# A third tile for the rows of a batch, another order of the first loads and scales, and one quarter's sums a quarter earlier

## The chip, the cores and the metric

The kernel runs on one core of one Trainium2 chip. The metric is the device time of one execution in microseconds (us), taken as the median of several runs. Beside it stands one execution recorded by the hardware profiler; all times inside the kernel come from that one, in us from the start of its span.

The engines are named as the profile names them: PE (TensorE) with PEld, its weight loads; DVE (VectorE); ACT (ScalarE); POOL (GpSimd); SP (SyncE), which issues most DMAs.

## The reference, cut to what matters

An RWKV-5 attention layer with a decaying state per head, and behind it a layer of eight experts of which each token uses one.

```python
batch, n_heads, seq, head_dim = (4, 8, 768, 48)
...
for t in range(S):
    kt, vt, rt = (k[:, :, t], v[:, :, t], r[:, :, t])
    cur = np.einsum('bhd,bhe->bhde', u[None] * kt, vt)
    y[:, :, t] = np.einsum('bhd,bhde->bhe', rt, state + cur)
    state = w[None, :, :, None] * state + np.einsum('bhd,bhe->bhde', kt, vt)
...
x = np.ascontiguousarray(attn_out.transpose(0, 2, 1, 3)).reshape(B * S, H * D)
...
logits = x @ w_gate
expert_idx = np.argmax(logits, axis=1)
...
for e in range(E):
    mask = expert_idx == e
    ...
    xe = x[mask]
    h = np.maximum(xe @ w1[e], 0.0)
    ye = h @ w2[e]
    out[mask] = gate_w[mask, None] * ye
```

There are 3072 tokens of 384 numbers, and each expert has 1024 hidden numbers. Everything is float32.

## The kernel before

**Attention.** The work is cut into 16 pairs: batch b and two heads, pair i = 4b + hp. A pair's 768 tokens are six chunks of 128. For each pair the kernel loads a tile `rk` (r and k, channels on partitions, three tiles in turn; `load_rk`, L91) and a tile `vk` (v and k, tokens on partitions, four tiles in turn; `load_vk`, L96). SP issues both. What is done with a pair:

- `scale` (L264, instruction at L266): DVE multiplies r and k by the powers of the decay in `TT`; the result is `RK`. `pairs` (L270, L272) multiplies r by k for the tokens' own term (`rp`), on POOL except for pair 0; `keys` (L274, L276) multiplies k in `vk` by the decay to the chunk's end (`Kd`), mostly on POOL.
- `p_own` (L279, PE at L285) sums `rp` with u, and `own_t` (L288, DVE at L289) turns the sums. `diag` (L300, ACT at L303) puts them on the diagonal of the score tiles `A`.
- `p_scores` (L291, PE at L297) multiplies keys by queries into the PSUM banks X01 and X23; `mask` (L305, DVE at L309 and L311) copies the half above the diagonal into `A`, in three pieces.
- `p_ds` (L315, PE at L320) makes each chunk's addition to the state from `Kd` and `vk`, `scan` (L323, DVE at L325) carries the state through the chunks, and `p_out` (L329, PE at L340 and L345) makes the output from `A`, `vk`, the states and `RK`. `out_t` (L348, ACT at L350) copies it to `yT`, `p_tr` (L356, PE at L358) turns it so that tokens stand on partitions, and `keep` (L361, ACT at L363 and L364) copies it into `xb`, the rows of a batch. There are two `xb` tiles (L252), taken in turn by batch.

When a batch is complete, `choose` (L368) picks each token's expert, `p_rank` and `slots` give the place among the expert's tokens, `gates` and `ids` finish the row, and `send` (L410, POOL at L412) writes rows from `xb` to the HBM tensor `rows` at those places, one chunk of 128 tokens at a time, spread over the next pairs by the table `sends` (L696 to L699). So a batch's `xb` is read by DMAs during the four pairs after it, while the next batch fills the other tile. A batch's pairs reach `keep` two pairs late: batch 2's first rows (pair 8) are kept in step 10.

The order on each engine is the order in which the program text issues its instructions; each engine works its own list off in that order and waits on semaphores. The steps are written out by hand: pair 0 in L701 to L731, then the loop over i from L732. In a step, PE runs own tokens, scores, p_tr of i-2, p_ds of i, and p_out of i-1. `turn` (a copy of one number on POOL) makes POOL wait for DVE's `scale` or `own_t` before it goes on. `p_fill` (L107) multiplies an identity by itself; its result is used by nobody.

**First loads.** L103 to L105 issue r, k and v, k of pairs 0, 1, 2 in the order rk0, vk0, rk1, vk1, rk2, vk2, after the small tile `wug` (L78).

**Experts.** After the last pair, each expert's tokens are loaded from `rows`. Two small early passes take the first 160 tokens of experts 0 and 1; eight late passes k = 0 to 7 take the rest (widths in L36). From k = 2 on, the first matrix product is done in a form with fewer products: `quarter` (L486) computes a quarter of the hidden units from five sums of weights per quarter, which `quarter_sums` (L533) makes on DVE, and from four sums of tokens, which `token_sums` (L544) makes. `quart[q]` is one tile per quarter, shared by all passes. The second product of pass k-1 runs after the first of pass k: `L2` (L554) for the tokens past the first 256, and `tokens_out` (L586) for the first 256, again with sums (`inner_sums`, `weight_sums`). `tokens_out` begins with four small DVE operations at L589 to L594, which make the places `it2` to which the rows are scattered (L675). Its products go to PSUM banks in turn; the last one writes the bank that the first one used, so it waits for `add(so[1], ...)` (L621).

The loop over passes (L895) mixes these by hand. While pass k >= 2 runs its quarters q, DVE also makes the sums of the next pass's quarter q-2 (L923 and L924); those of quarters 2 and 3 follow after the pass, behind `xT` and `token_sums` of the next one (L928 to L932):

```python
                    if q > 1:
                        late[k + 1].quarter_sums(q - 2)
...
            if ahead:
                late[k + 1].token_sums()
                for q in range(0 if k == 1 else 2, 4 if k < n - 2 else 3):
                    late[k + 1].quarter_sums(q)
```

Of the kernel before, what the change touches and what calls it, by code (L numbers as in the profile page):

```python
# [11 lines left out]
I32 = mybir.dt.int32  # L12
# [28 lines left out]
def bc(ap, shape):  # L41
    return ap.to_broadcast(shape)


def straight(tc, rk, vk, w, w1, w2, out, flag):
# [45 lines left out]
    def load_rk(i):  # L91
        if i < U:
            b, hp = divmod(i, HP)
            nc.sync.dma_start(rks[i % 3][0:KP], rk[b, hp].rearrange("h p u s -> (h p) u s")[0:KP])

    def load_vk(i):  # L96
        if i < U:
            b, hp = divmod(i, HP)
            nc.sync.dma_start(vks[i % 4], vk[b, hp])

    ident = cp.tile([128, 128], FP32, name="ident")
    make_identity(nc, ident)
# [146 lines left out]
    Ss = [ca.tile([128, D, G - 1], FP32, name=f"S{i}") for i in range(2)]  # L249
    own = [ca.tile([128, G, 32], FP32, name=f"own{i}") for i in range(2)]  # L250
    yTs = [ca.tile([128, 2, S // 2], FP32, name=f"yT{i}") for i in range(3)]
    xbs = [ca.tile([128, G, HP, Q], FP32, name=f"xb{i}") for i in range(2)]  # L252
    lg, sub, ex, eq = [ca.tile([128, G, E], FP32, name=n) for n in ("lg", "sub", "ex", "eq")]
    rko = ca.tile([128, G, E], FP32, name="rko")
    mx, se, m2 = [ca.tile([128, G], FP32, name=n) for n in ("mx", "se", "m2")]
# [5 lines left out]

        return c + 4 * h if c < 4 else 8 + 2 * h + c - 4

    def scale(i):  # L264
        hp, x = i % HP, rks[i % 3]
        nc.vector.tensor_tensor(RKs[i % 3][0:KP].rearrange("p u (c t) -> p u c t", t=C),  # L266
                                x[0:KP].rearrange("p u (c t) -> p u c t", t=C),
                                bc(TT[:, hp, :, None, :], [KP, 2, G, C]), op=ALU.mult)

    def pairs(i, eng=None):  # L270
        x = rks[i % 3]
# [88 lines left out]

    def keep(i):  # L361
        b, hp = divmod(i, HP)
        nc.scalar.copy(xbs[b % 2][:, 0:4, hp, :], trv[0])  # L363
        nc.scalar.copy(xbs[b % 2][:, 4:G, hp, :], trv[1])  # L364

    full = [128, G, E]

    def choose(b):  # L368
        oh = ohs[b % 2]
        nc.vector.tensor_reduce(lg, xbs[b % 2][:, :, :, 2 * D:].rearrange("p c a e -> p c e a"), axis=AX, op=ALU.add)  # L370
        nc.vector.tensor_reduce(mx, lg, axis=AX, op=ALU.max)
        nc.vector.tensor_tensor(sub, lg, bc(mx[:, :, None], full), op=ALU.subtract)
        nc.scalar.activation(ex, sub, func=ACT.Exp)

        nc.vector.scalar_tensor_tensor(out=eq, in0=sub, scalar=0.0, in1=bc(rev[:, None, :], full),
                                       op0=ALU.is_equal, op1=ALU.mult)
        nc.vector.tensor_reduce(m2, eq, axis=AX, op=ALU.max)
        nc.vector.tensor_tensor(oh, eq, bc(m2[:, :, None], full), op=ALU.is_equal)
# [10 lines left out]
                             skip_group_check=True)  # L389

    def slots(b):
        oh, xb = ohs[b % 2], xbs[b % 2]
        nc.vector.tensor_tensor(rko, rp, oh, op=ALU.mult)
        with nc.allow_low_precision("whole numbers below 2^24"):
            nc.vector.tensor_reduce(slot[b % 2], rko, axis=AX, op=ALU.add)

    def gates(b):
        xb = xbs[b % 2]
# [11 lines left out]
    def send(b, cs):  # L410
        for c in cs:
            s_ = nc.gpsimd.indirect_dma_start(  # L412
                out=rows[:, :], out_offset=bass.IndirectOffsetOnAxis(ap=slot[b % 2][:, c:c + 1], axis=0),
                in_=xbs[b % 2][:, c].rearrange("p a q -> p (a q)"), in_offset=None, bounds_check=E * N - 1, oob_is_err=False)
            tc.declare_no_dep(s_.ins, group="rows", reason="each token has a row of its own")
            tc.add_to_no_dep_group("rows", s_.ins)

    def ids(b):
        nc.gpsimd.iota(xbs[b % 2][:, :, :, 2 * D + 1].bitcast(I32), pattern=[[4 * C, G], [1, HP]], base=4 * S * b,
                       channel_multiplier=4)  # L420

    def p_count():
# [18 lines left out]
    class Pass:  # L441
# [144 lines left out]
        def tokens_out(self):  # L586

            nt, it2 = self.nt, self.it2
            nc.vector.tensor_scalar(out=vt[:, 0:nt], in0=pos2[:, 0:nt], scalar1=float(self.s0),  # L589
                                    scalar2=bp[:, self.k:self.k + 1], op0=ALU.add, op1=ALU.is_lt)  # L590
            nc.vector.memset(it2[:, 0:nt], 1 << 20)
            nc.vector.tensor_scalar(out=ia[:, 0:nt], in0=self.xg[:, 0:nt, 1].bitcast(I32), scalar1=2, scalar2=None,  # L592
                                    op0=ALU.logical_shift_right)
            nc.vector.copy_predicated(it2[:, 0:nt], vt[:, 0:nt], ia[:, 0:nt])  # L594

# [16 lines left out]
            def Sm(k):  # L612
                return lambda f: sums[k][:, f, :]
# [17 lines left out]
            def weigh(o, x, t):  # L631
                nc.scalar.activation(o, x, func=ACT.Copy, scale=g[:, t])
# [171 lines left out]
    nc.gpsimd.tensor_copy(turn, xbs[1][0:1, G - 1, 2, 0:1])  # L804
    send(B - 2, range(3, G))
    p_out(U - 1)
    out_t(U - 1)
# [86 lines left out]

    for k, p in enumerate(late):  # L895
        o = late[k - 1]
        ahead = k + 1 < n and k > 0
        if k == n - 1:
            o.inner_sums()
# [10 lines left out]
        else:  # L910

            if k < 2:
                if k:
                    o.inner_sums()
                for f in range(FT):
                    p.L1((f,))
                    if f % 2:
                        result(p, f)
            else:
                for q in range(4):  # L920
                    p.quarter(q)
                    o.inner_sums((q,))
                    if q > 1:  # L923
                        late[k + 1].quarter_sums(q - 2)  # L924
                    if k == 2 and q % 2:
                        result(p, 2 * q - 1)
                p.relus()
            late[k + 1].xT()  # L928
            if ahead:
                late[k + 1].token_sums()  # L930
                for q in range(0 if k == 1 else 2, 4 if k < n - 2 else 3):
                    late[k + 1].quarter_sums(q)  # L932
            if k == 0:
                okay()
# [528 lines left out]
```

## Time and profile before

| What | Value |
|---|---|
| Median of 3 runs | 373.71 us (371.86 to 374.47) |
| The profiled execution, its own time | 367.2 us |
| Its span | 365.3 us |
| PE busy | 353.3 us, 97% of the span |
| DVE busy | 261.5 us, 72% |
| POOL busy | 204.6 us, 56% |
| ACT busy | 142.7 us, 39% |
| Granted PE clock | 0.996 |
| HBM read and written | 53.29 MB and 11.40 MB, 177 GB/s over the span |

How to read the profile lines: in a timeline a line has start, duration, engine, source line, operation, written tile <- read tiles, the shape, and how many instructions of the kind were merged; in square brackets stands how long the engine had been idle and what ended that wait. Ends of matrix products are modelled, so their start and the distance between weight loads are the better measure. A line of the DMA view has the tensor, the queue, the number of issues, the size of one and the time from issue to landing. SPq is the issue of a DMA by SP and no work of an engine.

The attention part ends at about 118 us, the early passes at about 142 us, and the late passes fill the rest.

### The profile page before, as it was taken

The page shows a single profiled execution, that of the slowest core. Times are in us where ns is not written, and L with a number is a line of the kernel's source. Part 1 is how long each engine was busy: PE and PEld are TensorE (multiplying, and loading weights), DVE is VectorE, ACT ScalarE, POOL GpSimd, SP SyncE. Part 2 cuts the span into 40 slices and gives each one's busy share as a digit, 9 for nine tenths or more (in the row PEclk, how much of TensorE's full clock was granted, in tenths as well). Part 3 has the DMA queues.
Part 4 walks back from the last instruction along what each step waited for, and adds up shares of the span by engine and source line. Part 5 has one row for each costly group of instructions (what it writes and reads, how often), then busy time and mean ns, then how long its engine had stood idle before and what let it go on. Part 6 is the DMA issues. An engine that isn't in the chain of part 4 may idle for free.

```text
span 365.3 us, 9077 instructions
## 1 busy us (share of the span) xinstructions
PE 353.3 (97%) x3355; PEld 335.1 (92%) x3355; DVE 261.5 (72%) x653; ACT 142.7 (39%) x411; POOL 204.6 (56%) x242
## 2 busy tenths in 40 slices
PE   8999999999999999999999999999999999999991
PEld 8788888878889999999999999999999999999891
DVE  6988798887872258675797994896788688685531
ACT  2688787777784301323213312312221231122210
POOL 5389889898864521642107308805912941999341
PEclk9999999999999999999999999999999999999998
DMA  7999999986566974988358237525842943313301
GB/s 211 272 253 241 282 255 264 255 249 195 212 170 203 316 282 99 245 257 217 126 178 196 88 92 200 159 86 168 191 129 93 210 148 127 102 51 108 126 20 50
DMA packets 35205, 65.08 MB, mean 178 GB/s; under 512 B 18617, under 2 KB 19657, under 8 KB 35152
## 3 DMA queue, kind: packets, MB, share of 16 engines
q1 hardware_dynamic: 29648, 49.86, 50.3%
q0 software_dynamic: 3776, 9.84, 7.6%
q10 hardware_dynamic: 1728, 4.72, 3.7%
q8 instruction: 28, 0.46, 0.6%
q14 instruction: 25, 0.20, 0.2%
HBM read 53.29 MB, written 11.40 MB: 177 GB/s over the span
## 4 chain that ended last, share of the span: by engine, by line
PE 90%; DVE 2%; POOL 2%; issue 2%; DMA 1%; POOLq 0%; ACT 0%; DVEq 0%
PE X L501 12%; PE X L563 10%; PE X L479 8%; PE tr L603 7%; PE yps L603 7%; PE X L297 6%; PE yps L340 6%; PE yps L501 5%; PE tr L358 5%; PE yps L345 3%; PE tr L501 3%; PE dsb L501 3%; PE dsb L603 3%; PE yps L563 2%; PE dsb L320 2%
## 5 line engine op out<-in xcount | busy, mean ns | idle before, releaser
L675 POOL DMA_INDIRECT out_dram<-yo,ix x28 | 28.4, 1013 | 68.0 <-DVE ia L592 63.8
L303 ACT ACTIVATE A<-ident,own 128x128 f32<-128x128 f32 x192 | 57.9, 390 | 7.0 <-DVE own L289 6.6
L412 POOL DMA_INDIRECT rows<-xb,slot x24 | 30.3, 1262 | 12.0 <-issue 4.8
L563 PE MATMUL X<-hT,w2s 128*128 128x160 f32 (+5 forms) x288 | 36.5, 287 | 0.0
L563 PEld LDWEIGHTS X<-hT,w2s 128*128 128x128 f32 x288 | 36.2, 191 | 0.2
L603 PE MATMUL yps<-tums,sums 128*128 128x192 f32 x184 | 32.4, 326 | 0.0
L603 PEld LDWEIGHTS yps<-tums,sums 128*128 128x128 f32 x184 | 30.3, 190 | 0.0
L675 POOL DMA_INDIRECT out_dram<-yt,it x16 | 16.8, 1048 | 22.1 <-DVE so L621 10.9
L272 POOL TENSOR_TENSOR rp<-rk 112x768 f32<-112x768 f32 x15 | 28.8, 1919 | 0.0
L266 DVE TENSOR_TENSOR RK<-rk,TT 112x1536 f32<-112x1536 f32 x16 | 27.8, 1735 | 1.1 <-DMA rk<-in_rk_dram 0.9
L297 PEld LDWEIGHTS X<-RK 48*128 48x128 f32 x384 | 23.1, 187 | 5.3 <-issue 4.3
L297 PE MATMUL X<-RK 48*128 48x128 f32 x384 | 27.1, 283 | 0.2 <-DVE RK L266 0.2
L309 DVE COPY_PREDICATED A<-strict,X 128x512 f32<-128x512 int32 x32 | 23.3, 742 | 5.0 <-ACT A L303 4.9
L501 PE MATMUL X<-xT,w1s 128*128 128x208 f32 (+5 forms) x120 | 26.0, 331 | 0.0
L689 POOL TENSOR_TENSOR tums<-w2s,tums 128x384 f32<-128x384 f32 x24 | 24.7, 1031 | 0.4
L340 PE MATMUL yps<-A,vk 128*48 128x128 f32 x384 | 24.0, 274 | 0.0
L501 PEld LDWEIGHTS X<-xT,w1s 128*128 128x128 f32 x120 | 20.9, 190 | 0.0
L340 PEld LDWEIGHTS yps<-A,vk 128*48 128x48 f32 x384 | 20.2, 123 | 0.5
L637 ACT COPY so<-tr 128x192 f32<-128x192 f32 x7 | 2.2, 318 | 44.4 <-PE tr L603 44.4
L689 DVE TENSOR_TENSOR sums<-hT 128x512 f32<-128x512 f32 x16 | 17.1, 1066 | 3.2 <-ACT hT L481 3.2
L603 PE MATMUL tr<-w2s,hT 128*128 128x192 f32 x112 | 19.4, 326 | 0.0
L530 ACT ACTIVATE hT<-hT 128x416 f32<-128x416 f32 (+5 forms) x23 | 12.3, 536 | 17.9 <-DVE hT L522 17.8
(214 smaller groups left out, 828.2 us busy)
## 6 DMA issues: line engine op xcount, KB each, us to landing
w1s<-in_w_dram SPq DMA_DIRECT2D x36, 384.0 KB, 3.2
rk<-in_rk_dram SPq DMA_DIRECT2D x16, 672.0 KB, 10.2
w2s<-in_w_dram SPq DMA_DIRECT2D x24, 384.0 KB, 3.8
vk<-in_vk_dram SPq DMA_DIRECT2D x16, 528.0 KB, 5.6
w2s<-in_w_dram ACTq DMA_DIRECT2D x8, 384.0 KB, 5.6
xs<-rows SPq DMA_DIRECT2D x16, 169.0 KB, 5.3
w1s<-in_w_dram ACTq DMA_DIRECT2D x4, 384.0 KB, 3.3
rows<-zt SPq DMA_DIRECT2D x1, 1248.0 KB, 8.9
```

What stands on the lines that cost most here:

```text
L266: nc.vector.tensor_tensor(RKs[i % 3][0:KP].rearrange("p u (c t) -> p u c t", t=C), x[0:KP].rearrange("p u (c t) -> p u c t", t=C), bc(TT[: ...
L272: (eng or nc.gpsimd).tensor_tensor(rps[i % 2][0:KP], x[0:KP, 0], x[0:KP, 1], op=ALU.mult)
L297: nc.tensor.matmul(o, lhsT=r[q, 1, c * C:(c + 1) * C], rhs=r[q, 0, c * C:(c + 1) * C], start=True, stop=True, skip_group_check=True)
L303: nc.scalar.activation(A[:, place(c, h), :], ident, func=ACT.Copy, scale=own[i % 2][:, c, h:h + 1])
L340: nc.tensor.matmul(o(c, h), lhsT=v[:, c, h * D:(h + 1) * D], rhs=A[:, place(c, h), :], start=c < 2, stop=c == 0, skip_group_check=True)
L412: s_ = nc.gpsimd.indirect_dma_start(out=rows[:, :], out_offset=bass.IndirectOffsetOnAxis(ap=slot[b % 2][:, c:c + 1], axis=0), in_=xbs[b % ...
L479: nc.tensor.matmul(p[:, 0:self.n], lhsT=w1s[self.k % 2][f // 2][:, m, f % 2 * 128:(f % 2 + 1) * 128], rhs=self.t[:, m, 0:self.n], start=m ...
L501: nc.tensor.matmul(p[:, at * n:(at + 1) * n], lhsT=a, rhs=b, start=j == 0, stop=j == len(ab) - 1, skip_group_check=True)
L563: nc.tensor.matmul(p[:, 0:n], lhsT=w2s[self.k % 2][f // 2][:, f % 2, m * 128:(m + 1) * 128], rhs=self.h[:, f, self.c:self.n], start=f == 0 ...
L603: nc.tensor.matmul(p[:, at * Z:(at + 1) * Z], lhsT=a(f), rhs=b(f), start=f == 0, stop=f == FT // 2 - 1, skip_group_check=True)
L675: s_ = nc.gpsimd.indirect_dma_start(out=to[:, :], out_offset=bass.IndirectOffsetOnAxis(ap=at, axis=0), in_=x, in_offset=None, bounds_check ...
L689: (eng or nc.vector).tensor_tensor(o, a, b, op=how)
```

## The change

- **Rows of a batch.** `xb` has three tiles instead of two, and a batch takes tile b % 3.
- **First loads.** rk0 is loaded by two DMAs, each with half of the tokens; the order is rk0 (two halves), rk1, vk0, rk2, vk1, vk2.
- **Start of pair 0 and 1.** `scale(0)` is done in two halves, and the scores of the first two chunks are issued after the first half. The scores of chunks 4 and 5 move ahead of the last key decays. `scale(1)` stands ahead of `keys(0)` on DVE, so behind `own_t(0)`. The first two masks of pair 0 stand ahead of `scan(0)`. The fills are 12 instead of 17, and 6 and 3 around `p_ds(0)` instead of 8 behind the scores.
- **Sums of a quarter.** In pass k = 2 alone the next pass's sums of quarter q-1 (not q-2) follow quarter q, so only those of quarter 3 stay behind the pass.
- **Places.** In every `tokens_out` the four small operations for `it2` are issued behind `so[3]` and its two weighings, not at the beginning.

```diff
     def load_rk(i):
...
-            nc.sync.dma_start(rks[i % 3][0:KP], rk[b, hp].rearrange("h p u s -> (h p) u s")[0:KP])
+
+            for q in (slice(0, S // 2), slice(S // 2, S)) if not i else (slice(0, S),):
+                nc.sync.dma_start(rks[i % 3][0:KP, :, q], rk[b, hp].rearrange("h p u s -> (h p) u s")[0:KP, :, q])
...
-    for i in range(3):
-        load_rk(i)
-        load_vk(i)
+    load_rk(0)
+    load_rk(1)
+    load_vk(0)
+    load_rk(2)
+    load_vk(1)
+    load_vk(2)
...
-    p_fill(17, X01[1][:, 0, :])
+    p_fill(12, X01[1][:, 0, :])
...
-    xbs = [ca.tile([128, G, HP, Q], FP32, name=f"xb{i}") for i in range(2)]
+    xbs = [ca.tile([128, G, HP, Q], FP32, name=f"xb{i}") for i in range(3)]
...
-    def scale(i):
+    def scale(i, c0=0, c1=G):
         hp, x = i % HP, rks[i % 3]
-        nc.vector.tensor_tensor(RKs[i % 3][0:KP].rearrange("p u (c t) -> p u c t", t=C),
-                                x[0:KP].rearrange("p u (c t) -> p u c t", t=C),
-                                bc(TT[:, hp, :, None, :], [KP, 2, G, C]), op=ALU.mult)
+        nc.vector.tensor_tensor(RKs[i % 3][0:KP].rearrange("p u (c t) -> p u c t", t=C)[:, :, c0:c1],
+                                x[0:KP].rearrange("p u (c t) -> p u c t", t=C)[:, :, c0:c1],
+                                bc(TT[:, hp, :, None, :], [KP, 2, c1 - c0, C]), op=ALU.mult)
...
-        nc.scalar.copy(xbs[b % 2][:, 0:4, hp, :], trv[0])
-        nc.scalar.copy(xbs[b % 2][:, 4:G, hp, :], trv[1])
+        nc.scalar.copy(xbs[b % 3][:, 0:4, hp, :], trv[0])
+        nc.scalar.copy(xbs[b % 3][:, 4:G, hp, :], trv[1])
...
             weigh(so[4], so[3], 0)
             weigh(so[5], so[3], 1)
+            places()
             product(bd, 0, Sm(3), B_(1, 1))
...
-    scale(0)
+    scale(0, 0, G // 2)
+    p_scores(0, range(2))
+    scale(0, G // 2, G)
     pairs(0, nc.vector)
     key_decay(0, HP)
     state_decay()
-    p_scores(0, range(2))
     p_own(0)
...
-    keys(0, nc.vector)
     diag(0)
+    p_scores(0, range(4, G))
     p_key_decay(1, HP - 1)
     load_rk(3)
     scale(1)
+    keys(0, nc.vector)
+    p_fill(6, yps[0][:, 384:512])
     nc.gpsimd.tensor_copy(turn, RKs[1][0:1, 0, 0:1])
     pairs(1)
     keys(1)
     p_ds(0)
-    scan(0)
     mask(0, 0)
     mask(0, 1)
-    p_scores(0, range(4, G))
+    scan(0)
     mask(0, 2)
-    p_fill(8, yps[0][:, 384:512])
+    p_fill(3, yps[0][:, 384:512])
...
+        lag = 1 if k == 2 else 2
...
-                    if q > 1:
-                        late[k + 1].quarter_sums(q - 2)
+                    if q >= lag:
+                        late[k + 1].quarter_sums(q - lag)
...
-                for q in range(0 if k == 1 else 2, 4 if k < n - 2 else 3):
+                for q in range(0 if k == 1 else 4 - lag, 4 if k < n - 2 else 3):
                     late[k + 1].quarter_sums(q)
```

`places` is the block of L589 to L594, made a function and called where the diff shows it.

More of the change, by code (lines that the diff above doesn't have):

```diff
@@ L369, in choose @@
         oh = ohs[b % 2]
-        nc.vector.tensor_reduce(lg, xbs[b % 2][:, :, :, 2 * D:].rearrange("p c a e -> p c e a"), axis=AX, op=ALU.add)
+        nc.vector.tensor_reduce(lg, xbs[b % 3][:, :, :, 2 * D:].rearrange("p c a e -> p c e a"), axis=AX, op=ALU.add)
         nc.vector.tensor_reduce(mx, lg, axis=AX, op=ALU.max)
@@ L391, in slots @@
     def slots(b):
-        oh, xb = ohs[b % 2], xbs[b % 2]
+        oh, xb = ohs[b % 2], xbs[b % 3]
         nc.vector.tensor_tensor(rko, rp, oh, op=ALU.mult)
@@ L397, in gates @@
     def gates(b):
-        xb = xbs[b % 2]
+        xb = xbs[b % 3]
         nc.vector.tensor_reduce(se, ex, axis=AX, op=ALU.add)
@@ L413, in send @@
                 out=rows[:, :], out_offset=bass.IndirectOffsetOnAxis(ap=slot[b % 2][:, c:c + 1], axis=0),
-                in_=xbs[b % 2][:, c].rearrange("p a q -> p (a q)"), in_offset=None, bounds_check=E * N - 1, oob_is_err=False)
+                in_=xbs[b % 3][:, c].rearrange("p a q -> p (a q)"), in_offset=None, bounds_check=E * N - 1, oob_is_err=False)
             tc.declare_no_dep(s_.ins, group="rows", reason="each token has a row of its own")
@@ L418, in ids @@
     def ids(b):
-        nc.gpsimd.iota(xbs[b % 2][:, :, :, 2 * D + 1].bitcast(I32), pattern=[[4 * C, G], [1, HP]], base=4 * S * b,
+        nc.gpsimd.iota(xbs[b % 3][:, :, :, 2 * D + 1].bitcast(I32), pattern=[[4 * C, G], [1, HP]], base=4 * S * b,
                        channel_multiplier=4)
@@ L588, in tokens_out, with places @@
             nt, it2 = self.nt, self.it2
[L589 to L594, printed above, removed]
+            def places():
+                nc.vector.tensor_scalar(out=vt[:, 0:nt], in0=pos2[:, 0:nt], scalar1=float(self.s0),
+                                        scalar2=bp[:, self.k:self.k + 1], op0=ALU.add, op1=ALU.is_lt)
+                nc.vector.memset(it2[:, 0:nt], 1 << 20)
+                nc.vector.tensor_scalar(out=ia[:, 0:nt], in0=self.xg[:, 0:nt, 1].bitcast(I32), scalar1=2, scalar2=None,
+                                        op0=ALU.logical_shift_right)
+                nc.vector.copy_predicated(it2[:, 0:nt], vt[:, 0:nt], ia[:, 0:nt])
             h, ws, g = self.h, w2s[self.k % 2], self.xg[:, :, 0:1]
@@ L803, in straight @@
     keep(U - 2)
-    nc.gpsimd.tensor_copy(turn, xbs[1][0:1, G - 1, 2, 0:1])
+    nc.gpsimd.tensor_copy(turn, xbs[(B - 1) % 3][0:1, G - 1, 2, 0:1])
     send(B - 2, range(3, G))
```

## The prediction

> **What bounds the kernel now.** I read the page first (busy shares, then the chain that ended last), then the timeline of three places that the diff touches, then the landings of the first loads.
>
> ```profile
> PE 353.3 (97%) x3355; PEld 335.1 (92%) x3355; DVE 261.5 (72%) x653; ACT 142.7 (39%) x411; POOL 204.6 (56%) x242
> ...
> PE 90%; DVE 2%; POOL 2%; issue 2%; DMA 1%; POOLq 0%; ACT 0%; DVEq 0%
> ```
> TensorE works 353.3 of 365.3 us and carries 90% of the chain. Only its 12 us of holes can be won, and an edit on another engine pays only where it closes one. Three holes lie near the diff.
>
> Hole 1, the end of pass k=2 (timeline):
> ```profile
> 189.88 1.46 PE L603 MATMUL tr<-tums,sums 128*128 128x192 f32 x8
> ...
> 191.60 0.22 DVE L589 TENSOR_SCALAR vt<-pos,bp 128x2 int32<-128x2 f32 x1
> ...
> 192.01 0.35 DVE L621 TENSOR_TENSOR so<-dsb,so 128x192 f32<-128x192 f32 x1
> ...
> 192.51 1.54 PE L603 MATMUL dsb<-tums,hT 128*128 128x192 f32 x8 [1.16 <-DVE so L621]
> ```
> The last product overwrites bank dsb, which VectorE reads only at 192.01, because two quarters' sums (five operations each, 189.33 to 190.45 and on to 191.6) and four small operations (191.60 to 192.01) stand ahead of that read.
>
> Hole 2, pair 10:
> ```profile
> 78.47 0.33 ACT L364 COPY xb<-X 128x208 f32<-128x208 f32 x1 [2.04 <-DMA rows<-xb,slot]
> ...
> 78.69 0.86 ACT L350 COPY yT<-yps 112x384 f32<-112x384 f32 x2
> 79.23 1.12 PEld L358 LDWEIGHTS tr<-sel,yT 112*128 112x128 f32 x8 [0.74 <-ACT yT L350]
> 79.23 1.29 PE L358 MATMUL tr<-sel,yT 112*128 112x104 f32 x8 [0.55 <-ACT yT L350]
> ```
> Batch 2 writes the xb tile that batch 0 is still sending from; ScalarE waits for that DMA, and TensorE behind it.
>
> Hole 3, the start. The chain passes through POOL: rp at 13.24, then TensorE's own tokens at 15.11.
> ```profile
> 13.24 1.82 POOL L272 TENSOR_TENSOR rp<-rk 112x768 f32<-112x768 f32 x1
> ...
> 15.03 1.19 POOL L276 TENSOR_TENSOR Kd<-vk,T 128x480 f32<-128x480 f32 x1
> ...
> 17.09 0.66 PE L320 MATMUL dsb<-vk,Kd 128*48 128x48 f32 x20
> ...
> 21.11 1.77 DVE L266 TENSOR_TENSOR RK<-rk,TT 112x1536 f32<-112x1536 f32 x1
> 21.23 3.35 POOL L272 TENSOR_TENSOR rp<-rk 112x768 f32<-112x768 f32 x1
> ```
> To see: POOL's product takes 1.82 alone, but 3.35 when it starts just after VectorE's scale: it stands still until that ends (22.88). The loads issued at 2.67 (vk1) and 3.68 (rk2):
> ```profile
> rk<-in_rk_dram SPq DMA_DIRECT2D x1, 672.0 KB, 11.9
> vk<-in_vk_dram SPq DMA_DIRECT2D x1, 528.0 KB, 10.3
> ```
> So vk1 lands at 12.97 and rk2 at 15.58. Windows of 1 us show the DMA share at 0.94 to 1.13 from 3 us on: the queue is full, and what goes ahead pushes back what follows.
>
> [...] The trace agrees (3.35 against 1.82; the turn copies of 1.55 to 1.62 under L266 against 0.18). [...] The packet records agree: 21 ns at least for 416 bytes, 119 for 3072, 232 for 6144. [...] Here the first fill's weight loads stand 0.213 us apart until 7.58 and 0.112 after.
>
> **One quarter's sums sooner (with the small operations moved): -1.40 us.** For k=2 the lag is 1: the sums of quarter q-1 follow quarter q. Behind quarter 3 stands one set where two stood around the transposes: minus five operations, 189.33 to 190.45, 1.12 us. The four small operations go behind so[3]: minus 0.41. The read of dsb moves from 192.01 to 190.48, ends at 190.83, before the product ahead ends (191.34). The hole closes: weight loads of that product and the next start 2.76 us apart (189.72, 192.48), of which 1.30 is the normal distance (188.42 to 189.72), less 0.06 that the next is shorter: 1.40. After that TensorE is its own limit: the last final of the pass then ends near 193.5, and the next quarter's first midu isn't due before 194.1. The moved set is done after quarter 1, at 177.09, under quarter 2: it delays midu from 177.32 to about 178.2, whose next reader waited for TensorE until 179.01, so it is free; without that cover it would cost 1.12. Its weights need no new wait: the last issue of that load is at 159.3. The small operations behind so[3] lie in 0.35 to 0.64 us of idle time ahead of the next final, in the other passes too: 0. Bounds: 1.1 to 1.5.
>
> **Three xb tiles: -0.78 us.** Without the DMA, L364 waits for the mask that ends at 77.16, as in pair 6 (mask to 51.57, copy at 51.65): 77.24 for 78.47. L350 then ends by 78.4, and L358 starts behind the scores at 78.61, as in pair 6 to 7 (scores 51.92, L358 53.02). Saved 79.23 - 78.61 = 0.62, plus 0.16 as L358 to L320 took 1.67 there and 1.51 in pair 7. Check: pair 11 lasts 7.44 (scores 77.59 to 85.03), pair 7 6.55, less 0.11 for the count: 0.78. At pair 14 the copy waited for the mask too (103.57), so nothing is won. Bounds: 0 to 0.9. Moved addresses: nothing of the next pool starts before all sends land (134.80), as before.
>
> **The start: +0.65 us.** Two DMAs for one on SP's queue: 0.42 us more of issue ahead of the rest, done by some 5.1, before any is needed; rk3's issue only waits for rp(0), 8.7 for 9.43, in a queue that is full anyway. Packets of 1536 bytes: by the records 8.8 ns + bytes/27.4, four cost 26 ns more than one of 6144; 7 rows per engine make 0.18 us. Step by step:
> - Half of rk0 lands near 5.5 (6.71 less half of the 2.5 us between landings), tables ready 5.87: scale from 5.9 for 6.80, but halves cost 2 x 0.9 for 1.76 and the second lands near 6.9. rp ends 8.72 (9.43), own tokens 9.73 (10.44): 0.7 sooner.
> - rk1 is now second, landing near 9.4: scale(1) 9.65 to 11.4 (13.04). vk0 lands near 11.3: keys(0) to 12.0; [...] POOL's rp(1) runs 12.1 to 13.95 (15.06): 1.1 sooner. Masks, scan, last mask to 14.6; own tokens to 15.0; scale(2), rk2 there since 13.8, 14.9 to 16.65.
> - But vk1 now stands behind rk2: as many bytes ahead as rk2 had, so 15.58 + 0.18 = 15.75. keys(1) on POOL, ready at 15.03 before, [...] 16.65 to 17.85. p_ds(1) starts at 17.9 (17.09). Behind it on POOL: the turn copy, rp(2) (to 19.85) and keys(2); on TensorE p_out(0). From p_ds to the next own tokens it is 2.73 us (23.49 to 26.22): 20.63 for 19.98, a loss of 0.65. Later pairs are bound by TensorE (6.22 each), so it stays.
> - Fewer fills (12 for 17, 6 + 3 for 8) are hidden: TensorE waits anyway. Unknown: whether the array, its fill ending at 6.56, still doubles its clock at 7.58. I take yes, as the scores follow by 6.9; if not, its doubled work until 17.9 is mostly waited for anyway: up to 1 us more. Bounds: -1.0 (vk1 by 14.1, as the first engines brought rk2) to +1.6.
>
> **Sum.** -1.40 - 0.78 + 0.65 = -1.53 us on the profiled execution of 367.2 (span 365.3): 365.7. The median of the runs is 6.5 above it; the same distance gives 372.2.
>
> **Rivals.**
> 1. The start wins: vk1 lands [...] (by 14.9), or POOL is not held. For it: rp(1) is 1.1 us sooner. Against: the full queue. Then -0.3 to -1.0, say -0.6: 370.9.
> 2. The third tile does nothing, another wait ending at the same time: 373.0. Against: pair 6.
> 3. Slower: the half packets hold the queue. Lateness of vk1 is free until 16.65, 0.9 us, then counts in full; the gains are gone at 2.4 us of delay (vk1 at 18.2), and beyond, say 3.5 us, it gives 374.8. Against: 0.18 by the packet records.
>
> **Chances.** Forecast 0.64 (own range 371.2 to 373.2), rival 1 0.22, rival 2 0.08, rival 3 0.03, a cold array 0.03 (373.2). The runs of before spread over 2.6 us; with a third of that (0.9) at each end I go from 370.9 - 0.9 to 373.0 + 0.9: 370.0 to 373.9. Faster by over 1% (about what a measurement of this kernel can tell from no change; 3.7 us) needs more than all holes named, so rival 1's far end and luck: 0.10; slower 0.02; within 0.88.
>
> **What would show it.** No wait of TensorE on L621 near 190, and its product 1.3 us behind the one ahead. L364 of pair 10 right behind its mask. keys(1) on POOL ending near 17.9, about 1.2 or stretched under scale(2), and p_ds(1) later than 17.09: right for the start; p_ds(1) before 16.9 proves it wrong. Weight loads 0.112 apart after 7.6. The forecast falls if vk1 lands before 15, or if a later load is late, which the full queue could also bring.

## The result, and the profile after

| | before | changed |
|---|---|---|
| median of 20 runs each, us | 371.71 (369.72 to 377.36) | 375.38 (372.1 to 378.8) |
| ratio of the runs | | 1.0095, 95% interval 1.0068 to 1.0121 |
| profiled execution, own time and span, us | 367.2, 365.3 | 378.8, 376.8 |
| mean granted clock of TensorE in it | 0.996 | 0.979 |

The change makes the kernel slower by 0.9%; the forecast was 372.2, its range ended at 373.9. The changed kernel's profile is one of its longer executions, so its stages are compared, not its end alone.

The page of the changed kernel (busy times, granted clock in 40 slices of 9.4 us, the queue that brings instructions, the chain by engine):
```profile
PE 358.8 (95%) x3347; PEld 339.0 (90%) x3347; DVE 266.1 (71%) x654; ACT 142.5 (38%) x411; POOL 204.8 (54%) x242
...
PEclk9697999999999999999999999999999999999998
...
q8 instruction: 28, 0.46, 0.5%
...
PE 83%; issue 5%; POOL 4%; DMA 3%; DVE 2%; SPq 1%; ACT 0%; POOLq 0%; DVEq 0%
```
TensorE is busy for longer (358.8 for 353.3 us) with eight products fewer: in the second and fourth slice it ran at a lower clock (6 and 7 tenths, 9 on the page of before). 7% of the chain moved from PE to "issue", POOL and DMA.

The timeline of its start (start, duration, engine, line; in brackets the idle time before and what ended it):
```profile
6.71 0.71 PE L302 MATMUL X<-RK 48*128 48x128 f32 x8 [0.21 <-DVE RK L271]
9.08 0.63 PE L290 MATMUL dsb<-rp,wug 112*2 112x192 f32 x8 [1.65 <-DVE rp L277]
11.31 1.76 DVE L271 TENSOR_TENSOR RK<-rk,TT 112x1536 f32<-112x1536 f32 x1 [1.17 <-DMA rk<-in_rk_dram]
12.69 2.79 PE L115 MATMUL yps<-ident 128*128 128x128 f32 x12
13.74 1.85 DVE L281 TENSOR_TENSOR Kd<-vk,T 128x480 f32<-128x480 f32 x1 [0.67 <-DMA vk<-in_vk_dram]
15.65 0.86 PE L325 MATMUL dsb<-vk,Kd 128*48 128x48 f32 x20 [0.17 <-DVE Kd L281]
17.87 1.20 POOL L281 TENSOR_TENSOR Kd<-vk,T 128x480 f32<-128x480 f32 x1 [2.79 <-DMA vk<-in_vk_dram]
22.82 0.51 PE L290 MATMUL dsb<-rp,wug 112*2 112x192 f32 x8 [0.52 <-POOL rp L277]
23.26 1.38 PE L302 MATMUL X<-RK 48*128 48x128 f32 x19
26.09 0.75 PE L302 MATMUL X<-RK 48*128 48x128 f32 x5 [1.45 <-issue]
26.77 2.04 PE L363 MATMUL tr<-sel,yT 112*128 112x104 f32 x8
```
Three things stand here. Each of the loads behind the first ends a wait (second r, k at 11.31, first v at 13.74, second v at 17.87). TensorE pauses twice, 1.65 us ahead of the first own tokens and 1.45 us in the midst of 24 equal products. After each pause work takes longer: 12 products of the fill 2.79 us (16 took 2.05 before), eight turns 2.04 (1.14 before). The same in windows; the column after POOL is the granted clock, then the DMA share:
```profile
6.00:9.00 3.00, 1.22 (x13) 0.84 (x11) 3.00 (x4) 0.00 (x0) 1.65 (x10) 1.00 0.92 239
9.00:12.00 3.00, 2.92 (x25) 2.08 (x25) 1.69 (x4) 1.83 (x7) 0.00 (x0) 0.55 1.07 242
12.00:15.00 3.00, 3.00 (x16) 2.93 (x15) 2.33 (x2) 2.20 (x8) 1.86 (x2) 0.50 0.99 228
...
27.00:30.00 3.00, 3.00 (x22) 2.82 (x24) 0.09 (x1) 1.30 (x4) 1.51 (x2) 0.50 1.04 237
```
The clock comes up in the fill (at 5.9), falls to half at 9.3 for 6.8 us, and again at 26.4 for 6.8 us.

The two other places of the forecast, in the same timeline:
```profile
85.40 0.33 ACT L369 COPY xb<-X 128x208 f32<-128x208 f32 x1 [0.81 <-DVE se L404]
...
203.01 1.46 PE L610 MATMUL tr<-tums,sums 128*128 128x192 f32 x8
203.59 0.35 DVE L628 TENSOR_TENSOR so<-dsb,so 128x192 f32<-128x192 f32 x1
204.31 1.46 PE L610 MATMUL dsb<-tums,hT 128*128 128x192 f32 x8
```
Pair 10's copy no longer waits for the rows' DMA, and the product of pass 2 follows the one ahead after 1.30 us, with no wait for so. Both holes are closed. The step that this shortens is that of pair 11: 6.55 us for 7.32 from own tokens to own tokens. (The expectations below call it pair 10, which took 6.62 us in both.)

Where the time went, from the starts of the own tokens of pairs 3 and 15, of the first product with `quart`, and the end of the last product. Left: the two profiles on record; right: both kernels profiled once more (e5 and e16 below).

| stretch, us | before | changed | difference | e5 before | e16 changed | difference |
|---|---|---|---|---|---|---|
| start to pair 3 | 26.22 | 33.95 | +7.73 | 27.60 | 32.20 | +4.60 |
| pair 3 to pair 15 | 77.35 | 78.02 | +0.67 | 77.40 | 76.58 | -0.82 |
| to the first quarter | 65.22 | 69.95 | +4.73 | 65.22 | 65.22 | 0.00 |
| to the last product | 188.63 | 187.23 | -1.40 | 188.63 | 187.23 | -1.40 |
| sum | | | +11.73 | | | +2.38 |

The 4.73 us of the third stretch belong to the chip of the changed kernel's first profile, not to the change: the last section shows it. Nor do 1.44 us of the second belong to the change: pairs 8 and 12 took 0.33 and 1.11 us longer in that profile, which e16 lacks and all of e1 to e4, with either half of the change, have in part or whole. Without them the second stretch is 0.77 us shorter.

### The profile page after: what moved, and what is told of

The parts are those of the page before. It is cut to its first block, busy times and chain, and to the rows that moved or that the text cites. A ratio compares the mean times of both kernels' runs of the same rounds, so it can differ in the third digit from the quotient of the medians.

```text
span 376.8 us, 9061 instructions
## 1 busy us (share of the span) xinstructions
PE 358.8 (95%) x3347; PEld 339.0 (90%) x3347; DVE 266.1 (71%) x654; ACT 142.5 (38%) x411; POOL 204.8 (54%) x242
## 4 chain that ended last, share of the span: by engine, by line
PE 83%; issue 5%; POOL 4%; DMA 3%; DVE 2%; SPq 1%; ACT 0%; POOLq 0%; DVEq 0%
PE X L506 12%; PE X L568 9%; PE X L484 9%; PE yps L610 8%; PE tr L610 8%; PE yps L506 5%; PE X L302 4%; PE yps L345 4%; PE tr L363 3%; PE dsb L610 3%; PE tr L506 3%; PE dsb L506 3%; DMA vk<-in_vk_dram 3%; PE yps L568 2%; PE yps L350 2%
## 5 line engine op out<-in xcount | busy, mean ns | idle before, releaser
L417 POOL DMA_INDIRECT rows<-xb,slot x24 | 29.9, 1246 | 12.9 <-issue 5.1
L302 PEld LDWEIGHTS X<-RK 48*128 48x128 f32 x384 | 24.0, 193 | 7.0 <-issue 6.5
L271 DVE TENSOR_TENSOR RK<-rk,TT 112x1536 f32<-112x1536 f32 (+1 forms) x17 | 29.0, 1711 | 1.2 <-DMA rk<-in_rk_dram 1.2
L302 PE MATMUL X<-RK 48*128 48x128 f32 x384 | 28.3, 290 | 1.7 <-issue 1.5
L345 PE MATMUL yps<-A,vk 128*48 128x128 f32 x384 | 25.2, 283 | 0.0
L345 PEld LDWEIGHTS yps<-A,vk 128*48 128x48 f32 x384 | 21.4, 128 | 0.6
L363 PE MATMUL tr<-sel,yT 112*128 112x104 f32 x128 | 19.4, 296 | 1.9 <-ACT yT L355 1.3
L355 ACT COPY yT<-yps 112x384 f32<-112x384 f32 x32 | 13.9, 481 | 18.1 <-PE yps L350 9.1
L363 PEld LDWEIGHTS tr<-sel,yT 112*128 112x128 f32 x128 | 16.4, 199 | 4.4 <-ACT yT L355 1.5
L754 POOL COPY turn<-own 1x1 f32<-1x1 f32 x14 | 14.3, 1020 | 11.1 <-DVE own L294 9.4
```

The source lines that it names most:

```text
L302: nc.tensor.matmul(o, lhsT=r[q, 1, c * C:(c + 1) * C], rhs=r[q, 0, c * C:(c + 1) * C], start=True, stop=True, skip_group_check=True)
L345: nc.tensor.matmul(o(c, h), lhsT=v[:, c, h * D:(h + 1) * D], rhs=A[:, place(c, h), :], start=c < 2, stop=c == 0, skip_group_check=True)
L363: nc.tensor.matmul(trv[c // 4][:, c % 4, :], lhsT=yTs[i % 3][0:KP, c & 1, (c // 2) * C:(c // 2 + 1) * C], rhs=sel[:, c & 1, i % HP, :], st ...
L417: s_ = nc.gpsimd.indirect_dma_start(out=rows[:, :], out_offset=bass.IndirectOffsetOnAxis(ap=slot[b % 2][:, c:c + 1], axis=0), in_=xbs[b % ...
```

## The experiments

Theory A: both small edits gain what the forecast said, and the start loses more than that, by smaller packets in the first load (A1), by the order of loads and instructions (A2), and by the array's clock (A3). Theory B: the start costs about 0.65 us, and another edit costs 5 us elsewhere. A ratio is always against the kernel before, timed beside it on the same chip; chips differ by up to 1.3% (371.73 us for the kernel before on that of e1, 367.05 on that of e15). In words "e1" stands for the change without its start.

### One half of the change at a time (e1, e2)

e1 is the changed kernel with loads, fills and order of the start as before; e2 the kernel before with only these changed. Against the kernel before:

```diff
 e1, the two edits and nothing of the start
-    xbs = [... for i in range(2)]        with b % 2 where it is used
+    xbs = [... for i in range(3)]        with b % 3
-                    if q > 1:
-                        late[k + 1].quarter_sums(q - 2)
+                    if q >= lag:
+                        late[k + 1].quarter_sums(q - lag)
+            places()                     behind so[3], not first
 e2, the start and nothing else
-    load order rk0 vk0 rk1 vk1 rk2 vk2; p_fill(17), p_fill(8)
+    load order rk0 (two halves) rk1 vk0 rk2 vk1 vk2; p_fill(12), p_fill(6), p_fill(3); pairs 0 and 1 in the changed order
```

> The third tile and the earlier quarter's sums alone, with the loads, fills and order of the start as before. Theory A (both edits gain what the forecast said, 2.2 us, and the whole loss of 5.9 us sits in the start): 369.5, ratio 0.994. Theory B (the start costs about the 0.65 us of the forecast, and one of the two other edits costs some 5 us somewhere behind the pairs): 375, ratio 1.008. In its profile, A wants the own tokens of pair 2 at 19.98 and pair 10 lasting 6.6 us, not 7.3.

Measured: 370.29 for 371.73 us, ratio 0.9968 (0.9943 to 0.9993). Pair 11 takes 6.55 us; the own tokens of pair 2 come at 20.51.

> Only the start of the change (load order, first load in halves, scale in halves, fewer fills, moved scale, keys, scores), with two tiles and the old sums. Theory A: 377.6, ratio 1.016, slower than the changed kernel itself, with the granted clock at half in two stretches near 9 and near 26 us. Theory B: 372.4, ratio 1.002.

Measured: 378.07 us over 6 executions, 1.0154 (1.0105 to 1.0204); the clock is at half from 8.9 and from 26.0 us, for 6.8 us each. Theory B falls: the loss is all in the start. It is 1.27% (1.0095 less 0.9968), 4.7 us.

### The same on other chips (e5, e15, e16)

> The kernel before, unchanged, profiled once more beside the kernels of these experiments, so that their traces have one of the same day to stand against. All theories: a time of 369 to 375. If the two holes of the forecast are properties of the kernel, its profile shows pair 10 at 7.3 us with ScalarE waiting 2.0 us for the rows, and the product of pass 2 waiting 1.16 us for so; if they came from one execution, one or both are gone.

Measured: 368.52 us (median there 367.48). Its timeline has both holes again:
```profile
79.90 0.33 ACT L364 COPY xb<-X 128x208 f32<-128x208 f32 x1 [2.09 <-DMA rows<-xb,slot]
...
193.93 1.54 PE L603 MATMUL dsb<-tums,hT 128*128 128x192 f32 x8 [1.16 <-DVE so L621]
```

> The kernel of e1 once more, on the chip of e13 and e14. All theories: ratio 0.995 to 0.998; its profile has pair 10 at 6.6 us, the two last products of pass 2 at 1.3 us from each other, and, if the late signals of TensorE in the profiles of e1 to e4 belong to that chip and not to the kernel, none of those.

Measured: 365.89 for 367.05 us, 0.9963 (0.9941 to 0.9986); pair 11 6.55 us, the two products 1.30 us apart.

> The changed kernel itself, one profile on this chip. All theories: 371 where the kernel before takes 367.5. Theory A3: clock at half for 7 to 14 us near the start again. If the 4.7 us that the changed kernel's first profile lost between the early passes and the first quarter belong to its chip, they are gone here, and the product of pass 2 follows the one ahead after 1.3 us.

Measured: 370.86 us for the 367.05 of before; the table above has its stretches. Its timeline:
```profile
9.17 0.51 PE L290 MATMUL dsb<-rp,wug 112*2 112x192 f32 x8 [1.23 <-DVE rp L277]
...
22.55 1.38 PE L302 MATMUL X<-RK 48*128 48x128 f32 x19
25.88 0.60 PE L302 MATMUL X<-RK 48*128 48x128 f32 x5 [1.95 <-issue]
```
Both pauses come again, the second behind the same 19th product. The clock falls at 11.1 and at 28.1, for 3.4 us each.

### One part of the start alone (e6, e7, e8, e11)

Each is e1 with one part of the new start.

```diff
 e6   load_rk: two DMAs for i == 0, [.., slice(0, S // 2)] and [.., slice(S // 2, S)]
 e7   load_rk(0); load_rk(1); load_vk(0); load_rk(2); load_vk(1); load_vk(2)
 e8   the instructions of pairs 0 and 1 in the changed order (fills 6 and 3 for 8)
-e11  p_fill(17, X01[1][:, 0, :])
+e11  p_fill(12, X01[1][:, 0, :])
```

> The kernel of e1 (370.3) with only the first load split into halves; order of loads, fills and instructions as before. Theory A1 (the split makes the loads behind it about 2 us later, as between e3 and the changed kernel): the second r, k lands near 13.5 in place of 11.7, the second scale follows it, and the time rises by 1 to 2 us, to 371.8, ratio 1.000. Rival (the split costs 0.18 us as the forecast had it): 370.4, ratio 0.997, the second r, k landing near 11.9.

> The kernel of e1 (370.3) with only the order of the loads changed (second r, k ahead of first v, third ahead of second v), no halves, old fills, old order of instructions. Theory A2 (order of loads): first v near 11.6, where VectorE takes it at 11.2, second v near 15.6, where POOL takes it at 15.5: 0.5 to 1 us, 371.0, ratio 0.998. If the first v's delay stops TensorE long enough for the clock to fall (A3 on top of A2), 372.5 to 373.5, ratio 1.003.

> The kernel of e1 (370.3) with only the instructions of the first pair in the changed order (scale in halves, scores for the fifth and sixth chunk early, keys behind the second scale, scan behind two masks, 6 and 3 fills for 8), loads and the first 17 fills as before. If the new order needs the new loads and only the waits matter (A2): keys(0) 1.9 us later and pairs(1) behind it, about 0.5 us, 370.8, ratio 0.998. If it opens pauses of TensorE in which the clock falls (A3): 372.5 to 373.5, ratio 1.003, granted clock 0.985 to 0.988 in most runs.

> The kernel of e1 with only the first fill cut from 17 to 12 as in the change. The first r, k still lands whole near 7, so TensorE stands idle from 6.6 to about 8.8. Theory A3: this pause makes the clock fall for 3.4 to 6.8 us in nearly every execution, 1.3 to 2.6 us: ratio 1.002, mean clock 0.985. The forecast's view (fewer fills are hidden by the wait): 0.997.

| part alone | ratio | 95% interval | above e1's 0.9968 | executions at a mean clock of 0.991 or less |
|---|---|---|---|---|
| e6 halves | 1.0016 | 0.9993 to 1.0040 | 0.48% | 13 of 22 |
| e7 order of loads | 0.9981 | 0.9960 to 1.0002 | 0.13% | 11 of 19 |
| e8 order of instructions | 0.9991 | 0.9964 to 1.0018 | 0.23% | 15 of 22 |
| e11 12 fills for 17 | 1.0031 | 1.0017 to 1.0046 | 0.63% | 22 of 22 |
| e1, none | 0.9968 | 0.9943 to 0.9993 | | 7 of 22 |
| the changed kernel, all | 1.0095 | 1.0068 to 1.0121 | 1.27% | 20 of 20 |

The parts sum to 1.47%, all at once cost 1.27%. Each difference from e1 is uncertain by 0.3 to 0.4%, the sum by some 1.1%, so the two agree, but only loosely. Only e6 and e11 stand clear of e1, and these are the two that the forecast costed at 0.18 us and at nothing. e11's timeline shows the second:
```profile
1.44 4.41 PE L110 MATMUL X<-ident 128*128 128x128 f32 x24 [1.44 <-POOL ident masks.py:199]
9.99 1.23 PE L297 MATMUL X<-RK 48*128 48x128 f32 x8 [4.13 <-DVE RK L266]
```
The fill is over at 5.86, the first r, k is scaled only at 9.9, and the scores then take 1.23 us where e5, at full clock, takes 0.72. e11's profile has no second pause, so its loss is that of the fills and the clock. e6's own profile doesn't show its loss: that execution took 365.95 us, the lowest of its 22, and its second r, k landed at 12.29, no later than e5's at 12.53. Its cost rests on the times, and it isn't the clock's: the executions of e6 above 0.991 alone have a median of 367.44 us, 1.0009 of those of the kernel before, where the same ratio is 0.9951 for e1 and 0.9973 for e15.

### Taking one cost out of the changed kernel (e3, e4, e9, e13)

```diff
-e3   for q in (slice(0, S // 2), slice(S // 2, S)) if not i else (slice(0, S),):
+e3   nc.sync.dma_start(rks[i % 3][0:KP], rk[b, hp].rearrange("h p u s -> (h p) u s")[0:KP])
 e4   p_scores(0, range(2))
+e4   p_fill(8, yps[0][:, 384:512])
```

> The changed kernel with the first load of r and k in one DMA again, all else kept. If the 1536-byte packets and the extra DMA hold up the queue (theory A1), the second load lands some 2 us sooner than the 11.3 of the changed kernel's profile and the time falls to about 373, ratio 1.003. If the order of the loads, or the array's clock, is what costs (theories A2, A3), it stays at 375, ratio 1.009, or is worse by the later first scores.

Measured: 374.04 us, 1.0054 (1.0026 to 1.0083), 0.41% below the changed kernel. Its timeline:
```profile
8.15 0.71 PE L300 MATMUL X<-RK 48*128 48x128 f32 x8 [1.67 <-DVE RK L269]
...
15.76 1.20 POOL L279 TENSOR_TENSOR Kd<-vk,T 128x480 f32<-128x480 f32 x1 [0.57 <-DMA vk<-in_vk_dram]
```
The second v ends its wait at 15.76, not at 17.87. The pause of TensorE stays (1.67 ahead of the first scores), and the clock still falls.

> The changed kernel with 8 more fills between the first scores and the first own tokens, so that the array has no pause of 1.65 us near 7.4 us. Loads unchanged. If the fall of the clock to half is what costs (theory A3), the clock stays full from 6 us on and the time falls by 2 to 5 us, to 370.5 to 373, ratio 0.997 to 1.003. If late loads cost (A1, A2), TensorE only waits longer at full clock: 375, ratio 1.009.

Measured: 374.36 us, 1.0087 (1.0052 to 1.0122): no gain, and inconclusive, as 8 of 9 executions stay at a mean clock of 0.991 or less. The first fall is gone, but TensorE then waits 1.94 us for the first Kd and the clock falls at 15.8 instead. One bridge moves the pause.

e9 bridges both pauses:
```diff
     p_scores(0, range(2))
+    p_fill(8, yps[0][:, 384:512])
...
-    p_fill(6, yps[0][:, 384:512])
+    p_fill(15, yps[0][:, 384:512])
```

> The changed kernel with fills in both of its first pauses (8 between first scores and first own tokens, 15 in place of 6 where it waits for the first Kd), so that TensorE is busy without a pause until the loads are there. Theory A3 (the array's clock is the larger part of the loss): time at half clock falls from 12.0 us to 4 or 5 (ends of the run), and at 0.4 us lost per us at half clock the ratio falls from 1.0095 by 0.7 or 0.8 per cent to 1.002. Theory A2 (late loads are the larger part): the clock is full, but the ratio stays above 1.006.

Measured: 367.74 for 367.37 us, 1.0005 (0.9984 to 1.0026), 0.90% (3.3 us) below the changed kernel; 2 of 22 executions at a mean clock of 0.991 or less. Windows of its profile:
```profile
6.00:9.00 3.00, 2.19 (x21) 2.07 (x22) 2.81 (x3) 0.00 (x0) 1.74 (x10) 1.00 0.91 241
9.00:12.00 3.00, 3.00 (x37) 2.32 (x36) 1.66 (x4) 1.78 (x7) 0.00 (x0) 1.00 1.02 238
...
15.00:18.00 3.00, 1.93 (x35) 1.41 (x34) 3.00 (x5) 0.00 (x0) 0.21 (x1) 1.00 1.05 309
```
The loads are as late as in the changed kernel (second v at 18.0), but the clock is full until the products end, and the pause behind the 19th product is gone too. So the 3.3 us are what the fills take back in all, the clock's two falls and that pause together.

e13 is e9 with the first load in one DMA, as in e3, and 19, 5 and 10 fills for 12, 8 and 15:

> The changed kernel with the first load whole and with fills in its pauses (19 at the start, 5 before the first own tokens, 10 before the first Kd): the new order of loads and instructions without small packets and with a warm array. If the small packets are what e9 (1.0005) still loses against e1 (0.9968), this is at 0.996 to 0.998. If it is the new order of loads (second v later), it stays at 1.000.

Measured: 366.04 for 367.05 us, 0.9962 (0.9947 to 0.9977), 0.43% below e9 (0.26% either way) and level with e1. No execution of 22 at 0.991 or less. POOL in its timeline:
```profile
15.29 1.20 POOL L279 TENSOR_TENSOR Kd<-vk,T 128x480 f32<-128x480 f32 x1 [0.31 <-DMA vk<-in_vk_dram]
```
So the loss of 1.27% is taken apart from the other side: 0.90% by fills (the clock, and with it the second pause), 0.43% by the whole first load. The last step also changes the number of fills and the chip; e3 and e6, which change the first load alone, put it at 0.41 and 0.48%. The order of loads and instructions shows no cost when these are mended, and no gain.

### Packets, and more fills for the old start (e12, e10, e14)

Against e1:

```diff
+e12  for q in (slice(0, KP // 2), slice(KP // 2, KP)) if not i else (slice(0, KP),):
+e12      nc.sync.dma_start(rks[i % 3][q], rk[b, hp].rearrange("h p u s -> (h p) u s")[q])
-e10  p_fill(17, X01[1][:, 0, :]) ... p_fill(8, yps[0][:, 384:512])
+e10  p_fill(21, X01[1][:, 0, :]) ... p_fill(11, yps[0][:, 384:512])
+e14  p_fill(20, X01[1][:, 0, :]) ... p_fill(4, ...) behind p_key_decay(0, 1) ... p_fill(6, ...)
```

> The kernel of e1 with the first load in two DMAs of 56 rows each, so that its packets stay 6144 bytes and not 1536. The split by columns alone (e6) came out at 1.0016 against 0.9968 for e1. If it was the small packets, this one is at 0.997 to 0.998; if it was the second DMA itself (its issue, its lane, what it moves behind it), 1.001 to 1.002.

Measured: 365.85 us, 0.9973 (0.9950 to 0.9997). Two DMAs show no cost (e1, with one, has 0.9968); halves of rows do (e6, 1.0016).

> The kernel of e1 (third tile, earlier sums, old start) with 21 fills for 17 at the start and 11 for 8 ahead of the second pair. In e1 and in the kernel before a quarter to a third of the executions run below a mean clock of 0.99 and are 2.5 to 3 us longer. Theory A3: the longer fills take that part away: median 0.5 to 0.9 us below e1, ratio 0.995, few executions below 0.99. If the fills delay the first scores more than they save: 0.997 to 0.999.

> The kernel of e1 with 20 fills for 17 at the start, 4 more among the small products between first own tokens and first products of keys, and 6 for 8 behind them. e10 fell in the stretch of small products, not in the fill. If the clock counts how busy the array is in each stretch, this keeps it up in nearly all executions and takes 0.5 to 1 us off e1: ratio 0.995. If the narrow products or the phase decide, it is as e1, 0.997, with a quarter of the executions below a mean clock of 0.99.

Measured: e10 367.0 us, 0.9986 (0.9965 to 1.0008), 7 of 22 executions at 0.991 or less: more fills at the end of the wait did not help here. e14 366.04 us, 0.9960 (0.9939 to 0.9980), 2 of 22 against 3 of 15 for e15: too few to tell, and its median is e15's. Four versions beat the kernel before, e1 (e15), e12, e13 and e14, by 0.3 to 0.4%; their order can't be told.

## Why the prediction was wrong, step by step

- **What bounds the kernel, and the three holes: right.** e5 has all of them again.
- **One quarter's sums sooner, -1.40 us: right to the digit.** The stretch from first quarter to last product is 188.63 us in both profiles of before and 187.23 in both of the changed kernel.
- **Three tiles, -0.78 us: right in size (-0.82 in e16 against e5), wrong in what ends the wait next.** The forecast let the mask end it; it is `gates` (se, 0.81 to 0.83 us). The profile of before said so for pair 6, which the forecast went by: that copy, at 51.65, had waited 0.82 us for se, not for the mask. The size came out by luck, as in step 10 of the kernel before se ends only 0.08 us behind the mask (77.24 and 77.16).
- The two together give 2.2 us in the traces; the times of e1 and e15 show 1.2 to 1.4 us (0.32% and 0.37%, intervals down to 0.07% and up to 0.59%). 2.2 us are 0.6%, at or past the upper end of both intervals, so the times show less than the traces; where the rest goes was not found.
- **The start, +0.65 us: the step that failed. The times put it at 4.7 us** (0.0127 of 371.7): two of its terms were sized too small, one of them at nothing, and a pause of TensorE is not in it at all.
  1. *"Fewer fills ... are hidden: TensorE waits anyway."* What hides the fills' time doesn't hide their other effect. The forecast asked only whether the array would still double its clock, gave a failure 0.03 and at most 1 us; it did double, at 5.9 us. Nobody asked whether it would keep it. With 5 fills less and scores out early, TensorE is busy for 0.46 of the stretch from 5.9 to 9.3, and the clock falls. Alone that is 0.63% (e11), 2.3 us.
  2. *"7 rows per engine make 0.18 us."* With a whole first load the forecast's landings nearly come out: it said 9.4, 11.3 and 15.75 for the second r, k, the first v and the second v, and e3, e7 and e13 have 9.6 to 10.0, 11.4 to 11.6 and 15.2 to 15.6. In the five profiles with the new order and halves (changed, e2, e4, e9, e16) they are at 10.7 to 11.4, 12.9 to 13.7 and 17.0 to 18.0. So the second v is 1.4 to 2.9 us later by the halves, not 0.18; in time the term is 0.43% (e13 against e9), 1.6 us.
  3. *The pause behind the 19th product of pair 2* is in no term: 1.45 us (1.95 in e16), and the clock falls again behind it, at 26.4. Pair 2 took 11.13 us for 6.21: 1.45 are the pause, and some 3.4 are 6.8 us at half speed, where TensorE has no other wait; this doubled work was not "mostly waited for anyway". The fills of e9 took this pause away with both falls, 0.90% or 3.3 us in all; what the pause and the second fall are worth alone is not shown.
  4. keys(1) was not blocked by scale(2), as the steps had it by the author's estimate: it went first, at 17.87. scale(2) stood behind the own tokens of pair 1 till 18.41 and took 2.28 us (scale(1), at 11.31, took 1.76), and the own tokens of pair 2 came at 22.82, not 20.63. In e13, with the first load whole and the clock full, they come at 20.92 and p_ds(1) at 18.00 (forecast 17.9): without items 1 to 3 the forecast's times nearly hold, but not by its steps, as keys(1) goes first there too, at 15.29.
- **Rival 3 (slower) had part of the cause:** the halves do make the later loads late, but the second v, at 17.0 to 18.0, stays short of its break-even at 18.2. Another part was in the "cold array", which stood beside the rivals with 0.03. Each was judged alone, though the first makes the second likelier: a late load is a pause.
- **Carrying the profile's distance to the median (6.5 us) over:** the recorded execution of before is 4.5 us below the median of the 20 runs of the comparison, not 6.5, and that of the changed kernel 3.4 above. The distance is no constant. The lowest of the 20 runs of before is 369.72, and the recorded execution has none of the late signals of the last section; it may come from another chip, which is not on record.
- **What would show it:** two of the signs named did appear in the changed kernel's trace (no wait on so, p_ds(1) later than 17.09). The sign "weight loads 0.112 apart after 7.6" would have caught the fall; its failure says where to look.

Left open: why 1536-byte packets make the loads behind them late (their own times are as priced, 62 ns at the least where the forecast's line gives 65; the half packets are through by 6.5 us, and the first engine is on time behind them, 8.0 us in the changed kernel and in e3; it is the last that is late, 11.3 against 10.0). And what makes the second pause, 1.45 to 1.95 us "issue", behind the 19th of 24 products. It would fit a late fetch of TensorE's own instructions, though no trace shows whose instructions a fetch brings: the queue q8 "instruction" (28 packets of 16 KB) made its first fetch at 22.4 to 23.5 us in the four profiles with this pause (changed, at 23.23, e2, e3 with 0.52 us, e16), and at 15.3 to 21.1 in all others (before, at 16.84). (e8 and e14 have a like pause of 1.1 and 0.9 us, ending at 32.6 and 30.2, behind their second fetch.) The times fit closely: counted in TensorE's records of weight loads, products and waits, the places in e14 and in the changed kernel are some 256 apart (218 of a pair, 36 of the 18 products that e14's fills have more, 2 of one product), and the product there starts 2.70 to 2.97 us after the fetch ahead of it began in each of these six pauses (26.09 and 23.23 in the changed kernel), and never sooner in any profile. Why the fetch comes late was not found, and no run took that alone away.

## What to carry to other kernels

Work that only keeps TensorE busy is not free to cut because TensorE waits there (5 fills less cost 0.63% in e11): add up how busy it is left in each 3.4 us around the cut, for each fall at the start here lasted 3.4 to 10.2 us at half speed. A load that is split to start work sooner is split by rows, not inside them (e12 0.9973, e6 1.0016, e1 without a split 0.9968), and what it does to the loads behind it is measured, since here it was some ten times what the packets' own times gave (1.6 for 0.18 us). Two unlikely costs with one trigger are to be given a chance together.

## What the runs showed of the hardware

**The clock's windows.** In all 18 profiles the granted clock changes only at multiples of 3.41 us from its first change (in the changed kernel at 5.92, 9.33, 16.16, 26.40, 33.22 and 374.56), and a fall near the start lasts one, two or three of these. Pauses of 1.2 to 1.9 us came with falls (1.65 in the changed kernel, 1.94 in e4, 1.23 in e16). By the busy share of TensorE in the window ahead, near the start: at 0.46 or less the clock fell each time (changed, e2, e3, e4, e11); between 0.53 and 0.75 it fell in nine windows (one each in changed, e2, e7, e8, e10, e12 and e15, two in e16) and stayed up in others (0.57 in e1, 0.61 in e5, 0.67 in e6); at 0.76 and above it never fell. At the end of the run it stayed up behind windows of 0.42 to 0.47 (changed, e12, before). So the busy share of one window alone doesn't decide it. The windows that fell above 0.6 are full of narrow products (48 rows, or 2 columns), but so is one of 0.65 that stayed up (e16, from 21.3); what else decides is open.

**The old start falls too, by its phase.** 11 of the 41 executions of the kernel before that were timed beside e1 had a mean clock of 0.991 or less; their median is 373.93 us, that of the others 371.17. In the profiles of e12 and e15, whose clock comes up early (4.9 and 4.6 us), the 17 fills are done by 7.1 and the clock falls at 11.7 and 11.4; in e1, where it comes up at 6.0, they last until 7.7 and it stays up. Of the eight profiles with 17 fills, the four whose clock comes up at 5.8 or earlier fell, the four at 6.0 or later did not. A fill counted in products gets shorter when the clock comes up early (34 products took 5.67 us in e12, 6.21 in e1).

**The price of half clock.** Over the 41 executions the time rises by 0.36 us for each us at half clock (twice the missing share of the mean clock, times the span); over the 20 of the changed kernel by 0.42. Medians of the time at half clock: 4.4 us before, 12.0 changed; 7.6 times 0.4 is 3.0 us, near the 3.3 that e9 took back. What comes together with a fall, the second pause among it, is in that price.

**Signals of TensorE that come late on one chip.** In the changed kernel's timeline:
```profile
117.69 0.90 PE L350 MATMUL yps<-RK,S 48*48 48x128 f32 x20
118.52 1.90 PE L484 MATMUL X<-xTe,w1s 128*128 128x160 f32 x12
121.19 0.48 ACT L355 COPY yT<-yps 112x384 f32<-112x384 f32 x1 [3.86 <-PE X L484]
...
121.72 1.29 PE L363 MATMUL tr<-sel,yT 112*128 112x104 f32 x8 [1.30 <-ACT yT L355]
```
ACT may copy when L350 is done, near 118.6, and starts at 121.19: six signals of TensorE, due from 118.4 on, were recorded within 0.3 us from 121.16. This and like delays behind it made stretch three 4.7 us longer there, and 3.2 to 4.0 us longer in e1 to e4, which ran on one chip; on the chips of e5 to e16 it is 65.22 us in every profile. The kernel before took 371.7 us on the one and 367.0 to 367.5 on the others. Its reason was not found.
